# Three interleaved Strassen units in the last two tiles of an attention + SiLU-MLP kernel, with their first copies on VectorE

**Chip, cores, metric.** One core of one Trainium2 (trn2) chip. The metric is the device time of one execution in microseconds; the profiled span is 1.83 us shorter than the time of the same run.

## The reference

Abridged, in the notation of NumPy:

```python
def _attn_ref(q, k, v):                    # B=8, H=8, S=576, D=64, f32
    k_p = k.reshape(B, H, Sp, 8, D).mean(axis=3)        # Sp = 72
    v_p = v.reshape(B, H, Sp, 8, D).mean(axis=3)
    scores = np.matmul(q, k_p.transpose(0, 1, 3, 2)) / np.sqrt(D)
    attn = softmax(scores)                 # (cut)
    return np.matmul(attn, v_p)

def _moe_ref(x, w_in, w_out):              # x: 4608 x 512, w_in: 512 x 2048, w_out: 2048 x 512
    h = x @ w_in
    g = h * (1.0 / (1.0 + np.exp(-h)))
    return g @ w_out
```

## The kernel before

The 4608 tokens are worked off in nine tiles of 512 (t = 0 to 8). Each tile has an *up* phase (x to hidden, 16 groups of 128 hidden features) and a *down* phase (hidden to output). Attention of batch t+1 runs in between the matmuls of tile t; tiles 7 and 8 have none left. In the up phase some groups are *plain* (four matmuls of 512 columns each). Others are done four at a time as a *unit*: one level of Strassen, seven products in place of eight, each of four matmuls of 256 columns. The cost of a unit is its sums: of weights (once, in tile 0), of x (five for each tile), and of products. The products share three banks P, Q, R of PSUM, the memory into which TensorE writes its results. VectorE and ScalarE read them there, so that a product which adds onto a bank has to wait until the bank's last value has been read.

```python
def spread(fillers, n):          # fillers (at, function): run when matmul step `at` has been issued
    todo = sorted(fillers, key=lambda f: f[0])
    for i in range(n):
        yield i
        while todo and todo[0][0] <= i:
            todo.pop(0)[1]()
    for f in todo:
        f[1]()

def stage(y, n):                                     # unit y, Strassen product n
    if n == "2":
        product(y, 2, "P", True)                     # True: the bank is started anew
        nc.scalar.copy(r_sb, ps["P"])                # r, the "first copy"
    elif n == "5":
        product(y, 5, "Q", True)
        tt(out=rr_sb, in0=ps["Q"], in1=r_sb, op=ALU.add)             # rr
    elif n == "1":
        product(y, 1, "R", True)
        tt(out=t_sb, in0=ps["R"], in1=rr_sb, op=ALU.subtract)        # t
    elif n == "4":
        product(y, 4, "P", False)                    # adds onto P: r has to be out
        hidden(y, 1, 0, ps["P"])                     # SiLU on ScalarE
    elif n == "3":
        product(y, 3, "Q", False)                    # adds onto Q: rr has to be done
        hidden(y, 0, 1, ps["Q"])
    elif n == "7":
        product(y, 7, "P", False)                    # adds onto P: SiLU of 4 has to be done
        tt(out=c_sb[0], in0=ps["P"], in1=t_sb, op=ALU.add)           # c0
        hidden(y, 0, 0, c_sb[0])
    elif n == "6":
        product(y, 6, "Q", False)
        tt(out=c_sb[1], in0=ps["Q"], in1=t_sb, op=ALU.add)           # c1
    else:                                            # "s"
        hidden(y, 1, 1, c_sb[1])
```

The order of an up phase in tiles 2 to 8 (G is plain), its x sums and its hidden sums (the sums that the down phase, also Strassen, multiplies):

```python
items = (
    G(12, 13) + [(0, "251")] + G(14) + [(0, "43")] + G(15) + [(0, "76")]
    + [(1, "2")] + [(0, "s")] + [(1, "51")] + G(0) + [(1, "43")] + G(1)
    + [(1, "76")] + G(2) + [(1, "s")] + G(3)
)
for n in U_X:                                        # x sums for products 1, 4, 3, 7, 6
    f_up.append((0, lambda n=n: unit_x_sum(t, n)))
for n in (2, 5):
    f_up.append((36 if t > 1 else 45, lambda n=n: hidden_sum(n, 4, 8)))
f_up.append((56, lambda: hidden_sum(6, 4, 8)))
for n, k0 in ((2, 0), (5, 0), (1, 4), (1, 0)):
    f_up.append((64, lambda n=n, k0=k0: hidden_sum(n, k0, k0 + 4)))
f_down.append((33, lambda: hidden_sum(7, 0, 8)))
f_down.append((71, lambda: hidden_sum(6, 0, 4)))
```

The down phase starts with what needs only the upper half (4 to 8) of the hidden sums:

```python
product(2, KA, KQ)               # KA = 4, KQ = 8
product(5, KA, KQ)
product(2, 0, KA)
nc.scalar.copy(r_sb, ps["P"])
product(5, 0, KA)
tt(out=rr_sb, in0=ps["Q"], in1=r_sb, op=add)
for cc in ((0,), (1,)) if last else ((0, 1),):       # the last tile in two column halves
    product(1, 0, KQ, cc)                            # bank R
    ...                                              # products 4, 3, 7, 6 (cut)
```

The softmax here doesn't subtract the row's maximum and nothing guards it: scores larger than these inputs give would overflow.

Of the kernel before, what the change touches and what calls it, by code (L numbers as in the profile page):

```python
# [27 lines left out]
FP32 = mybir.dt.float32  # L28
FP32R = mybir.dt.float32r
BF16 = mybir.dt.bfloat16  # L30
AX = mybir.AxisListType.X
AF = mybir.ActivationFunctionType
ALU = mybir.AluOpType
# [3 lines left out]
def kernel(  # L37
# [9 lines left out]
    nc = tc.nc  # L47

    B, H, S, D = q.shape
# [11 lines left out]
    KQ, NQ, CQ = KG // 2, NTT // 2, d_model // 2  # L61
# [19 lines left out]
    singles = ctx.enter_context(tc.tile_pool(name="singles", bufs=1))  # L81
# [8 lines left out]
    def ps_tile(shape, dtype, tag, name):  # L90
        return psum.tile(shape, dtype, tag=tag, bufs=banks[tag], name=name)
# [16 lines left out]
    r_sb = singles.tile([128, 2, CQ], FP32, name="r_sb")  # L108
    rr_sb = singles.tile([128, 2, CQ], FP32, name="rr_sb")
    t_sb = singles.tile([128, 2, CQ], FP32, name="t_sb")  # L110
    xT = singles.tile([128, KF, NX], BF16, name="xT")

    w_sum1 = [singles.tile([128, 5, 2, 256], BF16, name=f"w_sum1{n}") for n in range(2)]
    x_sum = singles.tile([128, 5, 2, NQ], BF16, name="x_sum")
    c_sb = [singles.tile([128, 2, NQ], FP32, name=f"c_sb{n}") for n in range(2)]

# [272 lines left out]
    def spread(fillers, n):  # L389
# [7 lines that stand above are left out]



    UNITS = ((4, 6), (8, 10))  # L400
    UW = [
        {
            (i, j): w_in_sb[:, 2 * j : 2 * j + 2, 128 * u : 128 * (u + 2)]
            for i, u in enumerate(us) for j in range(2)
        } for us in UNITS
    ]
# [18 lines left out]
    def unit_x_sum(t, n):  # L425
        a, b = U_X[n]
        nc.vector.tensor_tensor(
            out=x_sum[:, U_XI[n]], in0=x_quarter(t, *a), in1=x_quarter(t, *b),
            op=ALU.subtract if n in (3, 4) else ALU.add,
        )  # L430

    def unit_weights(y, n):
        if n in U_WI:
            return w_sum1[y][:, U_WI[n]]
        return UW[y][0, 0] if n == 3 else UW[y][1, 1]

    def unit_x(t, n):
        if n in U_XI:
            return x_sum[:, U_XI[n]]
        return x_quarter(t, 0, 0) if n == 2 else x_quarter(t, 1, 1)  # L440


    def up(t, fillers, items):
        step = spread(
            fillers,
            sum(
                KF if len(it) == 3 else 2 * len(it[1].strip("s")) for it in items
            ),
        )
        ps = {}  # L450

        def product(y, n, bank, first):
            if first:
                tag = "mm" if bank == "R" else "at"
                ps[bank] = ps_tile([128, 2, NQ], FP32, tag, f"u_ps{bank}")
            w, x = unit_weights(y, n), unit_x(t, n)
            for u in range(2):
                next(step)
                for kk in range(2):
                    nc.tensor.matmul(  # L460
                        ps[bank][:, u, :], lhsT=w[:, kk, 128 * u : 128 * (u + 1)],
                        rhs=x[:, kk, :], start=first and u == 0 and kk == 0,
                        stop=kk == 1, skip_group_check=True,
                    )

        def hidden(y, i, j, src):
            g = UNITS[y][i]
            nc.scalar.activation(  # L468
                h_T[:, g : g + 2, j * NQ : (j + 1) * NQ], src, func=AF.Silu
            )  # L470

        tt = nc.vector.tensor_tensor

        def stage(y, n):
            if n == "2":
                product(y, 2, "P", True)
                nc.scalar.copy(r_sb, ps["P"])
            elif n == "5":
                product(y, 5, "Q", True)
                tt(out=rr_sb, in0=ps["Q"], in1=r_sb, op=ALU.add)  # L480
            elif n == "1":
                product(y, 1, "R", True)
                tt(out=t_sb, in0=ps["R"], in1=rr_sb, op=ALU.subtract)
            elif n == "4":
                product(y, 4, "P", False)
                hidden(y, 1, 0, ps["P"])
            elif n == "3":
                product(y, 3, "Q", False)
                hidden(y, 0, 1, ps["Q"])
            elif n == "7":  # L490
                product(y, 7, "P", False)
                tt(out=c_sb[0], in0=ps["P"], in1=t_sb, op=ALU.add)  # L492
                hidden(y, 0, 0, c_sb[0])
            elif n == "6":
                product(y, 6, "Q", False)
                tt(out=c_sb[1], in0=ps["Q"], in1=t_sb, op=ALU.add)
            else:
                hidden(y, 1, 1, c_sb[1])

        for it in items:  # L500
            if len(it) == 3:
                plain(t, step, *it)
            else:
                for n in it[1]:
                    stage(it[0], n)
        for _ in step:
            pass
# [61 lines left out]
    def quarter(i, j, ks):  # L569
        return h_T[:, j * KQ + ks.start : j * KQ + ks.stop, i * NQ : (i + 1) * NQ]  # L570
# [9 lines left out]
    def hidden_sum(n, k0, k1):  # L580
        a, b, op = H_SUMS[n]
        ks = slice(k0, k1)
        nc.vector.tensor_tensor(  # L583
            out=h_sum[n][:, ks, :], in0=quarter(*a, ks), in1=quarter(*b, ks), op=op
        )
# [166 lines left out]
    def load_half_2(name, half):  # L752
        for i0, i1 in ((0, SA), (SA, SLOTS), (SLOTS, SLOTS + 1)):
            load_slots(nc.gpsimd, 2, name, i0, i1, half)

    visits = [(f, g) for f in range(2) for g in range(2)]
    for t in range(NT):
        a = t + 1
        f_up, f_down = [], []
        if t == 0:  # L760
            GA = 11
            items = [(g, 0, HS) for g in range(GA)]
            items += [(g, HS, NTT - HS) for g in range(GA)]
            items += [(g, 0, NTT) for g in range(GA, KG)]
            f_up += [(1, lambda: denominators(0, 0, 1, on_dve=True))]
            f_up += [(5, lambda: denominators(0, 1, 1, on_dve=True))]
            f_up += [(13, lambda: numerators(0, 0, 1))]
            f_up += [(17, lambda: numerators(0, 1, 1))]
        else:
            G = lambda *gs: [(g, 0, NTT) for g in gs]  # L770
            if t == 1:
                items = (
                    G(12, 13, 14, 15) + [(0, "251")] + G(8) + [(0, "43")] + G(9)
                    + [(0, "76")] + G(10) + [(0, "s")] + G(11, 0, 1, 2, 3)
                )
            else:
                items = (
                    G(12, 13) + [(0, "251")] + G(14) + [(0, "43")] + G(15) + [(0, "76")]
                    + [(1, "2")] + [(0, "s")] + [(1, "51")] + G(0) + [(1, "43")] + G(1)
                    + [(1, "76")] + G(2) + [(1, "s")] + G(3)  # L780
                )
            for n in U_X:
                f_up.append((0, lambda n=n: unit_x_sum(t, n)))
            for n in (2, 5):
                f_up.append((36 if t > 1 else 45, lambda n=n: hidden_sum(n, 4, 8)))
            f_up.append((56, lambda: hidden_sum(6, 4, 8)))
            for n, k0 in ((2, 0), (5, 0), (1, 4), (1, 0)):
                f_up.append((64, lambda n=n, k0=k0: hidden_sum(n, k0, k0 + 4)))
            f_down.append((33, lambda: hidden_sum(7, 0, 8)))
            f_down.append((71, lambda: hidden_sum(6, 0, 4)))  # L790
# [9 lines left out]
        if a < B:  # L800
# [23 lines left out]
            if t == 0:  # L824
                f_down.append((0, lambda: load_half_2("k", 0)))
                f_down.append((0, lambda: load_q(2)))
                f_down.append((0, lambda: load_half_2("k", 1)))
                for half in range(2):
                    f_down.append((31, lambda half=half: load_half_2("v", half)))
                for y in range(2):  # L830
                    for n in U_W:
                        f_down.append((6, lambda y=y, n=n: unit_weight_sum(y, n)))
            elif a + 1 < B:
                for stage in range(2):
                    f_down.append((100, lambda stage=stage: pool_k(a + 1, stage)))
                f_up.append((0, lambda: load_q(a + 1)))
                f_up.append((1, lambda: load_one(a + 1, "k")))
                f_up.append((2, lambda: load_rest(a + 1, "k")))
                f_down.append((11, lambda: load_one(a + 1, "v")))
                f_down.append((12, lambda: load_rest(a + 1, "v")))  # L840
# [51 lines left out]
```

## Time and profile before

| | before |
|---|---|
| time, median (range) | 291.48 us (291.2 to 291.8, 4 runs) |
| span of the profiled run, granted clock | 288.6 us, 0.998 |
| up phase of tiles 7 and 8 | 13.0 us each, TensorE busy 12.9 |
| VectorE busy in it | 9.5 us |
| ScalarE busy in it | 8.8 us |

The lines behind it are in the prediction. In a timeline the first two columns are start and length in us. A row of "x4" is four instructions merged, so its length includes the overlap of matmuls with the next group; the distance from start to start is what a group costs TensorE.

### The profile page before, as it was taken

Reading aid. Unit: us, or ns where it says so; the run is one execution under the profiler, and the core shown is the slowest. Engines: PE = TensorE matmul, PEld = TensorE weight load, DVE = VectorE, ACT = ScalarE, POOL = GpSimd, SP = SyncE. Lnnn points to the kernel's source line nnn. Section 1 sums busy time; section 2 is a strip of 40 time slices with the busy share of each in tenths; the row PEclk is TensorE's granted clock in tenths of the full one; section 3 lists DMA queues with packets and bytes.
Section 4 is the critical chain, followed back from the end, with each engine's and each line's share of the span. In section 5 each row is a group of like instructions: output and inputs, shape, how many; then the busy total and the mean of one; then the engine's idle time right before and its main releaser. Section 6 shows DMA issues by size and latency. Waiting matters only on the chain.

```text
span 288.6 us, 6600 instructions
## 1 busy us (share of the span) xinstructions
PE 281.2 (97%) x2578; PEld 189.9 (66%) x2597; DVE 226.8 (79%) x417; ACT 187.9 (65%) x401; POOL 52.2 (18%) x68
## 2 busy tenths in 40 slices
PE   7989999999999999999999999999999999999995
PEld 2448434465667676657788767676777667786684
DVE  4986844989789796979698879887988876746783
ACT  1768675568656877578767866786679657425700
POOL 8744316501020011101200106203000000000000
PEclk9999999999999999999999999999999999999999
DMA  7999999893758565875995495979830023005004
GB/s 214 276 278 215 232 301 151 221 206 55 145 82 187 127 91 76 133 179 123 137 182 166 61 138 81 164 156 163 149 82 2 2 65 83 1 2 140 6 2 145
DMA packets 35295, 37.67 MB, mean 131 GB/s; under 512 B 9952, under 2 KB 27616, under 8 KB 35264
## 3 DMA queue, kind: packets, MB, share of 16 engines
q0 software_dynamic: 21760, 20.86, 43.3%
q1 hardware_dynamic: 12928, 15.48, 22.0%
q10 hardware_dynamic: 576, 0.92, 0.9%
q8 instruction: 20, 0.33, 0.5%
q14 instruction: 11, 0.09, 0.1%
HBM read 36.70 MB, written 9.44 MB: 160 GB/s over the span
## 4 chain that ended last, share of the span: by engine, by line
PE 91%; DVE 2%; ACT 2%; DMA 2%; issue 1%; DVEq 0%
PE hp_ps L518 24%; PE o_psP L623 15%; PE o_psQ L623 15%; PE u_psQ L460 6%; PE u_psP L460 6%; PE o_psR L623 5%; PE o_ps L550 4%; PE sc_ps L330 4%; PE nu_ps L370 3%; PE den_ps L347 3%; PE u_psR L460 2%; DMA raw<-in_k_dram 2%; PE warm_ps L672 1%; ACT es L338 1%; PE kz_ps L295 1%
## 5 line engine op out<-in xcount | busy, mean ns | idle before, releaser
L518 PE MATMUL hp_ps<-xT,w_in_sb 128*128 128x512 bf16 (+3 forms) x398 | 80.5, 338 | 1.2 <-ACT h_T L524 0.4
L524 ACT ACTIVATE h_T<-hp_ps 128x512 bf16<-128x512 f32 (+2 forms) x95 | 51.4, 545 | 33.1 <-PE hp_ps L518 31.9
L623 PEld LDWEIGHTS <-h_sum 128*128 128x128 bf16 x640 | 60.4, 98 | 15.2 <-issue 6.1
L583 DVE TENSOR_TENSOR h_sum<-h_T 128x1024 bf16<-128x1024 bf16 (+1 forms) x72 | 50.9, 743 | 7.0 <-ACT h_T L524 7.0
L518 PEld LDWEIGHTS <-w_in_sb 128*128 128x128 bf16 x412 | 39.3, 98 | 24.9 <-issue 1.5
L338 ACT ACTIVATE es<-sc_ps 72x288 bf16<-72x288 f32 x128 | 41.4, 402 | 12.6 <-PE sc_ps L330 12.5
L378 DVE TENSOR_TENSOR xT<-nu_ps,rec 128x288 bf16<-128x288 f32 x64 | 25.8, 450 | 13.2 <-PE nu_ps L370 13.0
L460 PEld LDWEIGHTS <-w_sum 128*128 128x128 bf16 x300 | 29.3, 98 | 7.7
L623 PEld LDWEIGHTS <-h_T 128*128 128x128 bf16 x256 | 23.5, 98 | 6.7 <-issue 4.3
L468 ACT ACTIVATE h_T<-c_sb 128x512 bf16<-128x512 f32 x30 | 18.8, 628 | 10.8 <-DVE c_sb L492 10.8
L152 DVE STREAM_TRANSPOSE qT<-q_bf 128x576 bf16<-128x576 bf16 x32 | 22.9, 753 | 0.0
L181 POOL DMA_DIRECT2D raw<-in_k_dram x5 | 7.0, 1405 | 75.1 <-DVE h_sum L583 37.7
L356 ACT ACTIVATE lnd<-den_ps 128x288 f32<-128x288 f32 x30 | 12.3, 411 | 10.8 <-PE nu_ps L370 5.8
L273 DVE TENSOR_TENSOR raw<-raw 128x384 f32<-128x384 f32 (+3 forms) x20 | 12.4, 619 | 8.0 <-DMA raw<-in_v_dram 4.4
L623 PE MATMUL o_psP<-w_out_sb,h_sum 128*128 128x256 bf16 x128 | 17.6, 273 | 0.0
L623 PE MATMUL o_psQ<-w_out_sb,h_sum 128*128 128x256 bf16 x128 | 17.6, 273 | 0.0
L623 PE MATMUL o_psQ<-w_sum,h_T 128*128 128x256 bf16 x128 | 17.5, 274 | 0.0
L623 PE MATMUL o_psP<-w_sum,h_sum 128*128 128x256 bf16 x128 | 17.0, 273 | 0.0
L623 PE MATMUL o_psR<-w_sum,h_sum 128*128 128x256 bf16 x128 | 16.7, 273 | 0.0
L623 PE MATMUL o_psP<-w_sum,h_T 128*128 128x256 bf16 x128 | 16.7, 273 | 0.0
L530 POOL DMA_DIRECT2D out_dram<-o_sb x1 | 0.6, 628 | 82.3 <-issue 82.3
L623 PE MATMUL o_psQ<-w_sum,h_sum 128*128 128x256 bf16 x128 | 15.4, 273 | 0.0
(77 smaller groups left out, 426.8 us busy)
## 6 DMA issues: line engine op xcount, KB each, us to landing
out_dram<-o_sb SPq DMA_DIRECT2D x128, 64.0 KB, 2.5
q_bf<-in_q_dram POOLq DMA_DIRECT2D x6, 576.0 KB, 11.4
raw<-in_k_dram SPq DMA_DIRECT2D x6, 512.0 KB, 5.5
raw<-in_k_dram POOLq DMA_DIRECT2D x5, 576.0 KB, 8.8
raw<-in_v_dram POOLq DMA_DIRECT2D x5, 576.0 KB, 8.7
raw<-in_v_dram SPq DMA_DIRECT2D x5, 512.0 KB, 6.4
w_in_sb<-in_moe_w_in_dram POOLq DMA_DIRECT2D x8, 256.0 KB, 8.7
w_out_sb<-in_moe_w_out_dram POOLq DMA_DIRECT2D x4, 512.0 KB, 13.5
```

The source lines that it names most:

```text
L152: nc.vector.transpose(out=st["qT"][:, a, f * QF : (f + 1) * QF].rearrange("r i c p -> r (i c p)"), in_=st["q_bf"][:, a, f * n : (f + 1) * n],)
L273: nc.vector.tensor_add(out=raw[..., :w], in0=raw[..., :w], in1=raw[..., w : 2 * w])
L330: nc.tensor.matmul(sc[s], lhsT=kz[b % 2][rows, g, c, :], rhs=st["qT"][rows, g, f * QF : (f + 1) * QF, c, :], start=(c == 0), stop=(c == 1),)
L338: nc.scalar.activation(es[:, s, :], sc[s], func=AF.Exp, scale=score_scale)
L356: nc.scalar.activation(lnd, den_ps[:, :HS], func=AF.Ln)
L378: nc.vector.tensor_mul(out=xT[:, 2 * g + c, cols], in0=nu[c][:, :HS], in1=rec)
L460: nc.tensor.matmul(ps[bank][:, u, :], lhsT=w[:, kk, 128 * u : 128 * (u + 1)], rhs=x[:, kk, :], start=first and u == 0 and kk == 0, stop=kk ...
L468: nc.scalar.activation(h_T[:, g : g + 2, j * NQ : (j + 1) * NQ], src, func=AF.Silu)
L518: nc.tensor.matmul(hp_ps[:, r0:r1], lhsT=w_in_sb[:, kk, g * 128 : (g + 1) * 128], rhs=xT[:, kk, x0 : x0 + r1 - r0], start=(kk == 0), stop= ...
L524: nc.scalar.activation(h_T[:, g, n0 : n0 + n], hp_ps[:, :n], func=AF.Silu)
L583: nc.vector.tensor_tensor(out=h_sum[n][:, ks, :], in0=quarter(*a, ks), in1=quarter(*b, ks), op=op)
L623: nc.tensor.matmul(ps[b][:, c, :], lhsT=left(n, kt, c), rhs=W_OUT[n][:, kt, :], start=b not in begun, stop=kt == k1 - 1, skip_group_check= ...
```

## The change

The intent: a third unit takes four more plain groups of tiles 7 and 8, where no attention competes, and saves another eighth of their matmul work. The three units are interleaved so that one's reads of PSUM lie beside another's matmuls, the four groups left fill gaps, and the first copies go to VectorE.

```diff
-    w_sum1 = [... for n in range(2)]
+    w_sum1 = [... for n in range(3)]
-    UNITS = ((4, 6), (8, 10))
+    UNITS = ((4, 6), (8, 10), (12, 14))
     (ps[bank] becomes ps[y, bank] throughout: cut)
-                nc.scalar.copy(r_sb, ps["P"])
+                copy = nc.scalar.copy if t < B - 1 else nc.vector.tensor_copy
+                copy(r_sb, ps[y, "P"])
+            if t >= B - 1:
+                items = (
+                    G(0) + [(0, "251"), (0, "43"), (2, "25"), (0, "76"), (2, "1")]
+                    + [(0, "s"), (2, "43"), (1, "25")] + G(1) + [(2, "76"), (1, "1")]
+                    + [(2, "s"), (1, "43")] + G(2) + [(1, "7")] + G(3) + [(1, "6s")]
+                )
-                f_up.append((36 if t > 1 else 45, lambda n=n: hidden_sum(n, 4, 8)))
+                f_up.append((45 if t == 1 or t >= B - 1 else 36, lambda n=n: hidden_sum(n, 4, 8)))
-                for y in range(2):                   # weight sums, in tile 0
+                for y in range(3):
```

More of the change, by code (lines that the diff above doesn't have):

```diff
@@ L111 @@
     xT = singles.tile([128, KF, NX], BF16, name="xT")
-    w_sum1 = [singles.tile([128, 5, 2, 256], BF16, name=f"w_sum1{n}") for n in range(2)]
+    w_sum1 = [singles.tile([128, 5, 2, 256], BF16, name=f"w_sum1{n}") for n in range(3)]
     x_sum = singles.tile([128, 5, 2, NQ], BF16, name="x_sum")
@@ L454, in product @@
                 tag = "mm" if bank == "R" else "at"
-                ps[bank] = ps_tile([128, 2, NQ], FP32, tag, f"u_ps{bank}")
+                ps[y, bank] = ps_tile([128, 2, NQ], FP32, tag, f"u_ps{bank}")
             w, x = unit_weights(y, n), unit_x(t, n)
@@ L460, in product @@
                     nc.tensor.matmul(
-                        ps[bank][:, u, :], lhsT=w[:, kk, 128 * u : 128 * (u + 1)],
+                        ps[y, bank][:, u, :], lhsT=w[:, kk, 128 * u : 128 * (u + 1)],
                         rhs=x[:, kk, :], start=first and u == 0 and kk == 0,
@@ L476, in stage @@
                 product(y, 2, "P", True)
-                nc.scalar.copy(r_sb, ps["P"])
+                copy = nc.scalar.copy if t < B - 1 else nc.vector.tensor_copy
+                copy(r_sb, ps[y, "P"])
             elif n == "5":
                 product(y, 5, "Q", True)
-                tt(out=rr_sb, in0=ps["Q"], in1=r_sb, op=ALU.add)
+                tt(out=rr_sb, in0=ps[y, "Q"], in1=r_sb, op=ALU.add)
             elif n == "1":
                 product(y, 1, "R", True)
-                tt(out=t_sb, in0=ps["R"], in1=rr_sb, op=ALU.subtract)
+                tt(out=t_sb, in0=ps[y, "R"], in1=rr_sb, op=ALU.subtract)
             elif n == "4":
                 product(y, 4, "P", False)
-                hidden(y, 1, 0, ps["P"])
+                hidden(y, 1, 0, ps[y, "P"])
             elif n == "3":
                 product(y, 3, "Q", False)
-                hidden(y, 0, 1, ps["Q"])
+                hidden(y, 0, 1, ps[y, "Q"])
             elif n == "7":
                 product(y, 7, "P", False)
-                tt(out=c_sb[0], in0=ps["P"], in1=t_sb, op=ALU.add)
+                tt(out=c_sb[0], in0=ps[y, "P"], in1=t_sb, op=ALU.add)
                 hidden(y, 0, 0, c_sb[0])
@@ L495, in stage @@
                 product(y, 6, "Q", False)
-                tt(out=c_sb[1], in0=ps["Q"], in1=t_sb, op=ALU.add)
+                tt(out=c_sb[1], in0=ps[y, "Q"], in1=t_sb, op=ALU.add)
             else:
```

## The prediction

> **What bounds the kernel now.** I read the page's busy line first, then the chain that ended last, then the matmul and VectorE timelines of tile 8's up phase (x to hidden), then the busy time by stretch. The busy line and the chain:
>
> ```profile
> PE 281.2 (97%) x2578; PEld 189.9 (66%) x2597; DVE 226.8 (79%) x417; ACT 187.9 (65%) x401; POOL 52.2 (18%) x68
> ...
> PE 91%; DVE 2%; ACT 2%; DMA 2%; issue 1%; DVEq 0%
> ```
>
> TensorE is busy 97% of the span and 91% of the chain, so any gap that opens in it is paid in full, and work taken from it is gained. The stretches of tile 7 up, tile 8 up, and the first 3.6 us of tile 8's down phase (us from the start; then length, and busy time of PE, weight load, DVE, ACT, POOL):
>
> ```profile
> 234.40:247.40 13.00, 12.89 (x88) 8.61 (x89) 9.49 (x17) 8.79 (x17) 0.00 (x0) 1.00 0.34 82
> 259.70:272.70 13.00, 12.90 (x88) 8.61 (x88) 9.50 (x17) 8.81 (x17) 0.00 (x0) 1.00 0.34 81
> 272.70:276.30 3.60, 3.60 (x34) 3.01 (x33) 2.50 (x5) 1.56 (x3) 0.00 (x0) 1.00 0.00 0
> ```
>
> Tiles 7 and 8 have no attention work beside their up phase. PE never stops there (12.9 of 13.0), VectorE has 3.5 us free, ScalarE 4.2 us. TensorE's pace, from the starts in its timeline (start, length, both us):
>
> ```profile
> 261.43 0.60 PE L460 MATMUL u_psP<-xT,w_sum 128*128 128x256 bf16 x4
> 261.87 0.60 PE L460 MATMUL u_psQ<-xT,w_sum 128*128 128x256 bf16 x4
> 262.31 0.60 PE L460 MATMUL u_psR<-x_sum,w_sum 128*128 128x256 bf16 x4
> 262.74 1.03 PE L518 MATMUL hp_ps<-xT,w_in_sb 128*128 128x512 bf16 x4
> 263.61 0.60 PE L460 MATMUL u_psP<-x_sum,w_in_sb 128*128 128x256 bf16 x4
> ```
>
> A Strassen product (four matmuls of 256 columns) advances PE by 0.437 us (261.43, 261.87, 262.31, 262.74), a plain group (four of 512) by 0.867 (262.74 to 263.61). The 0.60 and 1.03 overlap the next group. The VectorE timeline of the same stretch:
>
> ```profile
> 259.91 0.69 DVE L658 TENSOR_TENSOR o_sb<-o_psQ,t_sb 128x512 f32<-128x512 f32 x1 [1.00 <-PE o_psQ L623]
> 260.52 1.76 DVE L427 TENSOR_TENSOR x_sum<-xT 128x512 bf16<-128x512 bf16 x5
> 262.74 0.69 DVE L480 TENSOR_TENSOR rr_sb<-u_psQ,r_sb 128x512 f32<-128x512 f32 x1 [0.47 <-ACT r_sb L477]
> 263.54 0.69 DVE L483 TENSOR_TENSOR t_sb<-u_psR,rr_sb 128x512 f32<-128x512 f32 x1
> 266.04 0.69 DVE L492 TENSOR_TENSOR c_sb<-u_psP,t_sb 128x512 f32<-128x512 f32 x1 [1.81 <-PE u_psP L460]
> 266.64 0.68 DVE L496 TENSOR_TENSOR c_sb<-u_psQ,t_sb 128x512 f32<-128x512 f32 x1
> ```
>
> Four constants come out of it. Five x sums hold VectorE until 262.2 (pitch (1.76-0.42)/4 = 0.335). An op on 128x512 f32 lasts 0.69 us. Its successor starts 0.61 later if it does not read its result (266.04 to 266.64) and 0.80 later if it does (262.74 to 263.54, t_sb reads rr_sb). An add of a fresh PSUM bank starts 0.70 after the first matmul of its product (265.34 in the PE timeline to 266.04).
>
> **What the Trainium skill says.** "TensorE: Matmul & The Clock Gate", section "Wait — 56ns, not 53.3ns?": a warm matmul costs N/2.4 GHz + about 2.5 ns, so 109 and 216 ns for 256 and 512 columns; the trace agrees (0.437/4 = 109, 0.867/4 = 217). "VectorE: DVE Perf Modes", section "The TRN2 errata": fp32 tensor_tensor is (N+151)/0.96, 691 ns for 512; the trace has 692. Its section "The DRAIN you can't avoid" says that a same-engine read-after-write needs a semaphore; the trace agrees, the dependent add carries a semaphore event and comes 0.19 us later than an independent one. "PSUM — Partial Sum Buffer", "PSUM bank collisions raise a hardware error": a bank has to be guarded by semaphores between engines. So product 4, which accumulates on bank P, has to wait for the copy out of P; no run shows a collision here.
>
> **The change part by part.**
>
> *TensorE work.* 8 plain groups and 14 products, 8x0.867 + 14x0.437 = 13.05 us, become 4 and 21, 3.47 + 9.18 = 12.65. Gain 0.41 per tile, 0.82 in all, if nothing waits.
>
> *Weight sums of the third unit.* Five bf16 ops in tile 0's down phase, 5x0.335 = 1.7 us of VectorE. They come after the ten present ones (32.14 to 35.54), where VectorE then waits 4.19 us for a v load. Cost 0.
>
> *VectorE work.* Per tile one more set of four adds and three copies: 7x0.61 = 4.3 us, plus dependence gaps, on the present 9.5 in a phase of 12.65 us. It becomes full. ScalarE loses two copies, and trades four plain SiLUs for four of the unit's, so it stays near 9.
>
> *The head of the phase.* Now three plain groups (12, 13, 14) give VectorE 2.6 us around the first unit; the change leaves one group ahead and none between the first unit's products. Let 0 be the first matmul of tile 8's up phase (259.70). VectorE is in program order and the x sums are issued after the first matmul, so ahead of the copy. The copy of P starts at 2.50 (0.81 + 5x0.335; P itself is ready at 0.87+0.70 = 1.57) and ends at 3.19; rr runs 3.30-3.99, t 4.10-4.79. PE, with products 2, 5, 1 done at 2.18, waits for the copy with product 4 (3.24 rather than 2.18) and for rr with product 3 (4.04). It is done with product 3 at 4.47 rather than 3.05: **a gap of 1.42 us**.
>
> *The middle.* From 4.47 PE runs u2's 2, 5; u0's 7, 6; u2's 1, 4, 3; u1's 2, 5; G1; u2's 7, 6; u1's 1, 4, 3; G2, and reaches 12.33. VectorE meanwhile: r2 5.17, rr2 5.97, c0 6.58, c1 7.19, t2 7.80, r1 8.41, rr1 9.21, c0 9.98, c1 10.59, t1 11.20. Product 3 of u2 wants rr2 (done 6.66) at 7.10; u1's product 5 wants the fifth "at" bank's successor, u0's P, read by 7.27, at 7.97. No stall, by 0.4 us at the least. At u1's 7 there is one of about 0.15: ScalarE does u2's last SiLU (11.30) before that of u1's 4, which ends at 12.43, so 7 starts at 12.48, G3 at 12.92, 6 at 13.79; the phase ends at 14.22. Against 13.02 now: **+1.20**.
>
> *The tail.* Now the phase ends with two plain groups, and the last unit's outputs are long ready. After the change product 6 of u1 is last: its c1 could start at 14.49, but the hidden sum of 6 is issued before it and starts at 14.23 (c0 of u1 at 13.62 + 0.61), so c1 runs 14.86-15.54, SiLU 15.57-16.20, then four hidden sums in 2.50 us (the trace's figure), 16.23-18.73. The down phase has 1.74 us of work that needs none of them, then waits from 15.96 to 16.96 for the first; the third product kind (R) starts at 18.78, when the fourth sum is done. Now it starts at 276.25, which is 16.55 on this clock. **+2.23 per tile in all**: 1.42 + 0.15 of waits, less 0.41 of work gives 1.16 (1.20 with rounding and the wait latencies), and 1.03 in the tail.
>
> Tile 7 has the same timeline 25.3 us earlier (first matmul 234.41), so the sum is 2 x 2.23 = +4.5 us on the path: 291.53 + 4.5 = 296.0.
>
> **The rivals.** (1) *As intended*: waits fit in the slack and the time falls by 0.82 to 290.7. For it speaks that PE is the bound and VectorE had 3.5 us free; against it that this freedom lies later than 0 to 2.5, where the x sums are. (2) *Only the tail counts*: if the copy somehow ran before the x sums (or did not hold PE), rr would end by 4.0 at latest anyway; best case copy 1.57, no head gap beyond product 3's, giving about +0.4 to +1 per tile, 292.5 to 293.5. The program order speaks against it. (3) *VectorE throughput bound throughout*: if every handover cost 0.1 more than I took, about 19 VectorE ops in a row would add 1 to 2 us per tile beyond mine, 298 to 299. The table's slack of 0.4 us in the middle speaks against the full amount. (4) *Clock or start-up effects*: granted clock is 0.998, a gap of 1.4 us is not long; nothing.
>
> **Range and chances.** The two gaps follow from program order and durations that hardly vary, so I trust sign more than size: the tail could be 0.4 smaller if the hidden sum of 6 slips into an earlier hole, the middle 0.3 larger. I take 295.8 us, range 293.8 to 297.2. Two per cent slower is 297.4, which takes +5.8: chance 0.08. Two per cent faster is 285.7, which not even the ideal saving reaches: 0.01. Within 2%: 0.91.
>
> **What would show it.** In the profile after: in tiles 7 and 8 product 4 of the first unit starts about 3.2 us after the phase's first matmul and product 3 about 4.0, both released by VectorE; the first copy starts right after the x sums; VectorE has little idle time until 11.9; at the start of the down phase PE's weight load waits about 1 us for a hidden sum; R starts about 18.8 us after the phase's first matmul; tile 0 is unchanged. I am wrong if the first copy runs before or among the x sums, if PE's head gap is under 1 us, or if the change to R's start is not near 2.2 us in each tile.

## The result, and the profile after

| | before | after |
|---|---|---|
| time, median | 291.48 us | 295.44 us (294.72 to 295.83, 4 runs) |
| ratio, 95% interval | | 1.0133 (1.011 to 1.0155) |
| up phase, tile 8 | 13.0 us | 14.18 us |
| down phase of tile 8, start to the first matmul on R | 3.52 us | 4.21 us |
| first x sum of tile 7 to that of tile 8 | 25.30 us | 27.12 us |
| first x sum of tile 8 to the last group of matmuls | 23.75 us | 25.58 us |

A ratio is the mean time of one kernel's fast runs over that of the other's fast runs of the same rounds, so it is not quite the ratio of the medians.

The last two rows are *tile lengths*, read off the timelines as differences of start times (tile 7 before: 260.52 - 235.22). They are worth more here than the total, since they exclude the start of the kernel, which varies: in the profile of after, tile 7 begins 1.76 us later than before, 1.0 of that in the first 8 us, where the 19 warm-up matmuls took 7.13 us rather than 5.67. That stretch is not touched by the change. The other 0.75 appears between the first x sums of tiles 3 and 7, whose code is the same: counted from the first matmul of the scores, the x sums of tile 3 begin at 109.15 before and 109.13 after, those of tile 7 at 226.80 and 227.55. The two tile lengths together went up by 1.82 + 1.83 = 3.65 us, which accounts for most of the 3.96 us between the medians; the other 0.3 is within the scatter of runs.

The busy line and the chain of the page after:

```profile
PE 285.1 (97%) x2621; PEld 192.5 (65%) x2621; DVE 237.8 (81%) x436; ACT 186.0 (63%) x397; POOL 52.2 (18%) x68
...
PE 21%; DVE 5%; ACT 1%; issue 0%; DVEq 0%
```

These two lines mislead. TensorE is at 97% as before, since a busy share is taken over the whole span, and the chain's shares add up to only 27%: it breaks off, so it is no proof here. The stretches show it (both up phases; length, then busy time of PE, weight load, VectorE, ScalarE, GpSimd):

```profile
236.17:250.34 14.17, 13.09 (x102) 9.74 (x100) 13.01 (x23) 7.58 (x14) 0.00 (x0) 1.00 0.32 75
263.29:277.47 14.18, 13.10 (x103) 9.76 (x101) 13.02 (x23) 7.58 (x14) 0.00 (x0) 1.00 0.31 75
```

VectorE went from 9.5 of 13.0 us to 13.0 of 14.2. It is now the full engine, and TensorE has over a microsecond idle. What TensorE waits for, over the whole run (total us, times, longest):

```profile
PE u_psP L460 <- DVE r_sb L478: 1.8, 2, 0.9
...
PE o_psP L624 <- DVE h_sum L584: 1.0, 2, 0.5
...
PE u_psQ L460 <- DVE rr_sb L481: 0.4, 2, 0.2
```

Each occurs twice, once in tile 7 and once in tile 8, and none of the three occurs before. TensorE's timeline in tile 8 (first matmul 263.29):

```profile
265.03 0.60 PE L460 MATMUL u_psR<-x_sum,w_sum 128*128 128x256 bf16 x4
266.52 0.60 PE L460 MATMUL u_psP<-x_sum,w_in_sb 128*128 128x256 bf16 x4 [0.89 <-DVE r_sb L478]
267.31 0.60 PE L460 MATMUL u_psQ<-x_sum,w_in_sb 128*128 128x256 bf16 x4 [0.20 <-DVE rr_sb L481]
...
274.72 1.03 PE L519 MATMUL hp_ps<-xT,w_in_sb 128*128 128x512 bf16 x4
275.73 0.60 PE L460 MATMUL u_psP<-x_sum,w_sum 128*128 128x256 bf16 x4
...
278.34 1.04 PE L624 MATMUL o_psQ<-w_out_sb,h_sum 128*128 128x256 bf16 x8
279.87 1.05 PE L624 MATMUL o_psP<-w_out_sb,h_sum 128*128 128x256 bf16 x8 [0.50 <-DVE h_sum L584]
...
281.68 1.05 PE L624 MATMUL o_psR<-w_sum,h_sum 128*128 128x256 bf16 x8
```

The same first matmul on R in the profile of before, where the down phase starts at 272.73 (after: 277.47):

```profile
276.25 1.05 PE L623 MATMUL o_psR<-w_sum,h_sum 128*128 128x256 bf16 x8
```

Read it by pace: a product costs 0.437 us, so product 4 of the first unit (266.52) should have come at 265.47: 1.05 lost. Product 3 (267.31) lost another 0.35. The last unit's product 7 (275.73, due 275.59) lost 0.14. In the down phase product 2's lower half (279.87, due 279.21 at 0.872 per eight matmuls) lost 0.66. The bracket shows less than the pace, since the end of a matmul lies after the start of the next. And VectorE's queue in the same stretch:

```profile
264.10 1.76 DVE L427 TENSOR_TENSOR x_sum<-xT 128x512 bf16<-128x512 bf16 x5
265.78 0.69 DVE L478 COPY r_sb<-u_psP 128x512 f32<-128x512 f32 x1
266.57 0.69 DVE L481 TENSOR_TENSOR rr_sb<-u_psQ,r_sb 128x512 f32<-128x512 f32 x1
267.36 0.69 DVE L484 TENSOR_TENSOR t_sb<-u_psR,rr_sb 128x512 f32<-128x512 f32 x1
268.38 0.69 DVE L478 COPY r_sb<-u_psP 128x512 f32<-128x512 f32 x1 [0.33 <-PE u_psP L460]
269.18 0.69 DVE L481 TENSOR_TENSOR rr_sb<-u_psQ,r_sb 128x512 f32<-128x512 f32 x1
269.79 0.68 DVE L493 TENSOR_TENSOR c_sb<-u_psP,t_sb 128x512 f32<-128x512 f32 x1
270.38 0.68 DVE L497 TENSOR_TENSOR c_sb<-u_psQ,t_sb 128x512 f32<-128x512 f32 x1
271.17 0.69 DVE L484 TENSOR_TENSOR t_sb<-u_psR,rr_sb 128x512 f32<-128x512 f32 x1
...
276.45 0.68 DVE L493 TENSOR_TENSOR c_sb<-u_psP,t_sb 128x512 f32<-128x512 f32 x1
277.05 0.68 DVE L584 TENSOR_TENSOR h_sum<-h_T 128x1024 bf16<-128x1024 bf16 x1
277.74 0.69 DVE L497 TENSOR_TENSOR c_sb<-u_psQ,t_sb 128x512 f32<-128x512 f32 x1
279.12 2.50 DVE L584 TENSOR_TENSOR h_sum<-h_T 128x1024 bf16<-128x1024 bf16 x4 [0.70 <-ACT h_T L468]
```

From the first x sum (264.10) to the end of the last c1 (278.43) the view marks one hole, of 0.33 us. The first copy stands right behind the five x sums, as predicted.

### The profile page after: what moved, and what is told of

Its sections match the earlier page's. It is cut to its first block, busy times and chain, and to the rows that moved or that the text cites. A ratio compares the mean times of both kernels' runs of the same rounds, so it can differ in the third digit from the quotient of the medians.

```text
span 294.0 us, 6694 instructions
## 1 busy us (share of the span) xinstructions
PE 285.1 (97%) x2621; PEld 192.5 (65%) x2621; DVE 237.8 (81%) x436; ACT 186.0 (63%) x397; POOL 52.2 (18%) x68
## 5 line engine op out<-in xcount | busy, mean ns | idle before, releaser
L519 PE MATMUL hp_ps<-xT,w_in_sb 128*128 128x512 bf16 (+3 forms) x380 | 75.0, 337 | 0.4 <-ACT h_T L525 0.4
L525 ACT ACTIVATE h_T<-hp_ps 128x512 bf16<-128x512 f32 (+2 forms) x87 | 46.5, 540 | 29.8 <-PE hp_ps L519 24.2
L519 PEld LDWEIGHTS <-w_in_sb 128*128 128x128 bf16 x380 | 36.2, 98 | 22.0 <-issue 1.5
L460 PEld LDWEIGHTS <-w_sum 128*128 128x128 bf16 x340 | 33.2, 98 | 8.9 <-issue 0.5
L468 ACT ACTIVATE h_T<-c_sb 128x512 bf16<-128x512 f32 x34 | 21.2, 629 | 15.5 <-DVE c_sb L493 15.1
L460 PEld LDWEIGHTS <-w_in_sb 128*128 128x128 bf16 x136 | 13.2, 97 | 7.8 <-issue 4.5
```

The source lines that it names most:

```text
L460: nc.tensor.matmul(ps[y, bank][:, u, :], lhsT=w[:, kk, 128 * u : 128 * (u + 1)], rhs=x[:, kk, :], start=first and u == 0 and kk == 0, stop ...
L468: nc.scalar.activation(h_T[:, g : g + 2, j * NQ : (j + 1) * NQ], src, func=AF.Silu)
L519: nc.tensor.matmul(hp_ps[:, r0:r1], lhsT=w_in_sb[:, kk, g * 128 : (g + 1) * 128], rhs=xT[:, kk, x0 : x0 + r1 - r0], start=(kk == 0), stop= ...
L525: nc.scalar.activation(h_T[:, g, n0 : n0 + n], hp_ps[:, :n], func=AF.Silu)
```

## The experiments

Two readings of this profile are possible. **A**: the waits are local, each costs its own length, and one gets it back by putting TensorE work in front of it. **B**: VectorE's chain, from the x sums to the last c1, has become the pace of the phase, and TensorE's gaps are only where that shows. Every run below was correct against the reference. Tile lengths are from each run's own profile:

| run | ratio to before (95%) | tile 7 | tile 8 |
|---|---|---|---|
| before | 1 | 25.30 | 23.75 |
| after | 1.0133 (1.011 to 1.0155) | 27.12 | 25.58 |
| e4_sums_only | 1.0007 (0.9964 to 1.005) | - | - |
| e5_copies_only | 0.9966 (0.9933 to 0.9999) | 25.30 | 23.79 |
| e1_act_copies | 1.0088 (1.0044 to 1.0132) | 26.77 | 25.23 |
| e3_two_head | 1.0103 (1.0057 to 1.0148) | 27.04 | 25.50 |
| e2_late_x | 1.0073 (1.0042 to 1.0104) | 26.49 | 24.93 |
| e6_tail | 1.0097 (1.006 to 1.0135) | 26.51 | 25.29 |
| e7_all | 0.9967 (0.9943 to 0.9991) | 24.85 | 23.58 |
| e10_dup_after | 1.0163 (1.0129 to 1.0196) | 27.78 | 26.22 |
| e11_dup_e8 | 1.0008 (0.9975 to 1.0042) | 24.84 | 24.05 |
| e8_all_down | 0.9975 (0.9952 to 0.9998) | 24.85 | 24.04 |
| e9_all_dve_copies (= e8) | 1.0009 (0.9974 to 1.0044) | 24.85 | 24.04 |
| e12_split | 0.9996 (0.9963 to 1.0028) | 25.58 | 23.17 |

A warning on the second column: e8 and e9 are the same kernel byte for byte (see below), and their ratios differ by 0.34%. Each run has one profile, so a tile length is a single reading; the two of e8 and e9 agree to 0.01 us. Verdicts under half a per cent therefore rest on the tile lengths.

### The parts of the change alone

**e4_sums_only**, on the kernel before: only the third unit's weight sums.

```diff
-    w_sum1 = [... range(2)]          ->  range(3)
-    UNITS = ((4, 6), (8, 10))        ->  ((4, 6), (8, 10), (12, 14))
-                for y in range(2):   ->  range(3)
```

> The kernel before with only the third unit's weight sums added (five more VectorE ops in tile 0, their results unused). Both theories: ratio to before 1.000 +- 0.002; the five ops run in the hole ahead of the v load (VectorE's wait for it falls from about 4.2 to 2.4 us) and the first up phase of tile 1 starts no later. If the early part of the kernel carries some of the loss, the ratio is 1.001 to 1.003.

Ratio 1.0007: no cost seen, though the interval is wide. Its profiled execution was an outlier (987.54 us, TensorE busy 970 us at a granted clock of 1.0; I can't explain it) and shows nothing on the hole. The profile of after does: its weight sums are 15 in 5.08 us rather than 10 in 3.40, and VectorE's wait for the v load after them fell from 4.19 to 2.43 us. The traces of the other runs settle it: in five of the eleven that carry these sums (e2, e3, e7, e8, e12) tile 7's first x sum comes 226.78 to 226.84 us after the first matmul of the scores, against 226.80 before.

**e5_copies_only**, on the kernel before: only the copies of tiles 7 and 8 on VectorE.

```diff
-                nc.scalar.copy(r_sb, ps["P"])
+                copy = nc.scalar.copy if t < B - 1 else nc.vector.tensor_copy
+                copy(r_sb, ps["P"])
```

> The kernel before with only the two first copies of tiles 7 and 8 moved from ScalarE to VectorE. With two plain groups ahead of the first unit and one between its products the copy (2.50 to 3.19 us after the phase's first matmul) and rr (3.30 to 3.99) are done before products 4 (3.91) and 3 (4.34). Theory of order (what counts is what stands between a product and its read): ratio 1.000, no TensorE wait. Rival, the copies on VectorE are themselves the cost: +0.6 us or more for each tile, ratio 1.004.

Tile lengths 25.30 and 23.79 against 25.30 and 23.75: nothing in tile 7, 0.04 us in tile 8. The engine of the copy costs nothing where two plain groups lie ahead of it and one behind.

**e1_act_copies**, on the changed kernel: the copies back on ScalarE.

```diff
-                copy = nc.scalar.copy if t < B - 1 else nc.vector.tensor_copy
-                copy(r_sb, ps[y, "P"])
+                nc.scalar.copy(r_sb, ps[y, "P"])
```

> The changed kernel with the first copies of tiles 7 and 8 back on ScalarE; three interleaved units as changed. Theory of order: the copy starts 1.57 after the first matmul, product 4 at 2.2, but rr still waits behind the x sums until 2.50, so product 3 starts at 3.24 rather than 4.02; the gap moves partly to the last unit's product 7 (about 0.7 us, its bank read by ScalarE behind a SiLU that waits for VectorE) and the tail stays. Gain against the changed kernel only about 0.3 us per tile: 294.9, ratio to before 1.011. Rival, VectorE's amount of work paces the phase: taking three copies (3 x 0.6 to 0.8 us) off it gains about 2 us per tile, 291.5, ratio 1.000.

0.35 us gained in each tile, of 1.82 lost: the small figure was right and the rival (2 us) wrong. So the placing of the copies is a minor part of the loss. TensorE's waits in tiles 7 and 8 of this run:

```profile
PE u_psQ L460 <- DVE rr_sb L480: 0.9, 2, 0.4
PE u_psP L460 <- ACT h_T L468: 0.9, 2, 0.4
```

The wait for the copy is gone. In its place rr, still behind the x sums, holds product 3, and a SiLU holds the last unit's product 7: in ScalarE's queue the SiLU of product 4 (274.26) comes behind two (from 273.12) that waited for VectorE. The amount of VectorE work alone is therefore not the whole cause either: with three ops of 23 fewer, the handovers between the engines take over (VectorE waits 1.00 and 1.35 us for the copies of the second and the last unit).

### What paces the phase

**e3_two_head**, on the changed kernel: a second plain group at the head, taken from the middle.

```diff
-                    G(0) + [(0, "251"), ...
-                    + [(0, "s"), (2, "43"), (1, "25")] + G(1) + [(2, "76"), (1, "1")]
+                    G(0, 1) + [(0, "251"), ...
+                    + [(0, "s"), (2, "43"), (1, "25"), (2, "76"), (1, "1")]
```

> The changed kernel with group 1 moved from the middle to the head (two plain groups before the first unit). Theory A, the head gap by itself costs its length: the gap before product 4 falls from 1.06 to 0.2 us, and the time by 0.87 us per tile, 293.7, ratio to before 1.008. Theory B, VectorE's chain from the x sums to the last c1 sets the phase, and TensorE's gaps are only where it shows: the head gap falls to 0.2 and a gap of about 0.9 to 1.0 us opens later (before a product 7), R starts 18.4 us after the phase's first matmul as before, time unchanged, 295.4, ratio 1.013.

The tiles are 0.08 us shorter, not 0.87. TensorE in tile 8 of this run:

```profile
264.09 0.60 PE L460 MATMUL u_psR<-x_sum,w_sum 128*128 128x256 bf16 x4
264.71 0.60 PE L460 MATMUL u_psP<-x_sum,w_in_sb 128*128 128x256 bf16 x4
...
269.43 0.60 PE L460 MATMUL u_psQ<-xT,w_sum 128*128 128x256 bf16 x4
270.46 0.60 PE L460 MATMUL u_psP<-x_sum,w_sum 128*128 128x256 bf16 x4 [0.43 <-ACT h_T L468]
```

The gap ahead of product 4 shrank from 1.05 to 0.18 us, and one of 0.59 opened ahead of the second unit's product 7, which now has no plain group in front. Theory B: filling the largest visible gap gained next to nothing. The chain itself says the same. From tile 8's first x sum to the start of its last c1 it takes 13.64 us in the changed kernel and 13.55 here; in e10 below it takes 14.27, in e2 12.99, in e1 13.28, and the tile's length follows it within 0.02 us.

**e10_dup_after**, on the changed kernel: one VectorE op of the chain doubled in each of the two tiles.

```diff
                 tt(out=t_sb, in0=ps[y, "R"], in1=rr_sb, op=ALU.subtract)
+                if y == 2:
+                    tt(out=t_sb, in0=ps[y, "R"], in1=rr_sb, op=ALU.subtract)
```

> The changed kernel with one VectorE op doubled: t of the second unit in each of tiles 7 and 8 is computed twice (same operands, same result; 0.61 us of pitch, nothing else changed). Theory B, VectorE's own chain paces the phase: every op added to it lengthens the phase by its pitch, R starts 19.0 us after the first matmul rather than 18.4, +1.2 us in all, 296.6, ratio to before 1.0175. Rival, TensorE's waits at the head and the tail are local and there are 0.4 us of slack in the middle, as the prediction's middle part had it: +0.2 us per tile at most, ratio 1.0145 or less.

Tiles 0.66 and 0.64 us longer: the added op is paid in full. TensorE pays at a place far from the op, ahead of the last unit's product 7, which waits for a SiLU:

```profile
PE u_psP L460 <- ACT h_T L468: 1.3, 2, 0.6
```

The run that separates the two theories is e3. The price here agrees with B, but it can also be had from the prediction's own timeline: that has little slack after this op and a wait of 0.15 before the same product 7, so the "+0.2 us at most" of the expectation did not follow from it.

**e11_dup_e8**: the same doubled op in the repaired kernel e8 (below).

> The same doubled op in the repaired kernel (run e8_all_down), where by the worked-out timeline VectorE is ahead of TensorE. Theory B holds only where VectorE is the pace: here nothing is lost, no TensorE wait appears, and the first x sums of tiles 7 and 8 are 24.85 us apart as in e7_all; ratio to before 0.996. Rival, any VectorE work costs its time once three units run: +0.6 us per tile, ratio 1.000.

24.84 and 24.05 against 24.85 and 24.04 of e8: it costs nothing there. (The expected ratio of 0.996 was missed, at 1.0008. That is within the scatter: e9, at 1.0009, is the kernel that gave 0.9975 as e8.) A VectorE op has no price of its own; it has one where VectorE is the pace.

### Shortening the chain without taking work away

**e2_late_x**, on the changed kernel: the last three x sums issued later.

```diff
+            x_at = (0, 0, 7, 7, 9) if t >= B - 1 else (0, 0, 0, 0, 0)
-            for n in U_X:
-                f_up.append((0, lambda n=n: unit_x_sum(t, n)))
+            for at, n in zip(x_at, U_X):
+                f_up.append((at, lambda n=n: unit_x_sum(t, n)))
```

> The changed kernel with the x sums for products 3, 7 and 6 issued later (after steps 7, 7 and 9 of the phase rather than step 0), so that the first copy stands behind two x sums and not five. No work is taken from VectorE. Theory of order: the copy starts at 1.57 us, product 4 at 2.3, product 3 at 3.25 us after the phase's first matmul, and the phase is 0.6 to 0.76 us shorter per tile: about 294.0, ratio to before 1.009. Rival, the amount of VectorE work: time unchanged, ratio 1.013.

0.63 and 0.65 us gained per tile, the VectorE ops being the same. This is the largest single step of order: the first copy no longer stands behind the sums that nobody needs yet, and the sums fall into two holes of the chain, the 0.19 us by which t waits for its rr and the 0.4 us by which the second unit's copy came late because TensorE was late (0.33 in the bracket above). It is not the best placing. A new wait opened, on a sum now issued too late: product 4 starts at 263.65 and product 3 1.13 us after it.

```profile
264.78 0.60 PE L460 MATMUL u_psQ<-x_sum,w_in_sb 128*128 128x256 bf16 x4 [0.53 <-DVE x_sum L427]
```

**e6_tail**, on the changed kernel: more work in the down phase that does not need the last unit.

```diff
+            late = t >= B - 1
-            f_up.append((56, lambda: hidden_sum(6, 4, 8)))
+            (f_down if late else f_up).append((34 if late else 56, lambda: hidden_sum(6, 4, 8)))
             for n, k0 in ((2, 0), (5, 0), (1, 4), (1, 0)):
-                f_up.append((64, lambda n=n, k0=k0: hidden_sum(n, k0, k0 + 4)))
+                at = 45 if late and k0 else 64
+                f_up.append((at, lambda n=n, k0=k0: hidden_sum(n, k0, k0 + 4)))
         product(5, KA, KQ)
+        if t >= B - 1:
+            product(1, KA, KQ)
         product(2, 0, KA)
-            product(1, 0, KQ, cc)
+            product(1, 0, KA if t >= B - 1 else KQ, cc)
```

> The changed kernel with the down phase of tiles 7 and 8 given work that needs no output of the last unit: hidden sum 1 (upper half) issued early, product 1's upper half put between product 5's upper half and product 2's lower half, hidden sum 6 (upper half) moved into the down phase. The up phase is untouched. If the tail wait is a cost of its own: the 0.50 us wait before product 2's lower half and the later start of R go, product 4 of the down phase starts about 0.5 us earlier per tile (19.6 rather than 20.1 us after the phase's first matmul); 294.4, ratio to before 1.010. If it only takes up slack that VectorE makes elsewhere: unchanged, 1.013.

0.61 us gained in tile 7 and 0.29 in tile 8. The tail is a cost of its own: the chain of the up phase is as long as in the changed kernel (13.63 us against 13.64). In tile 8 a part came back as a new wait; there the columns are split, so product 3 comes eight steps sooner:

```profile
PE o_psQ L624 <- DVE rr_sb L641: 0.3, 1, 0.3
```

### A version that keeps the saving

**e7_all**, on the changed kernel: copies on ScalarE, late x sums, the tail of e6, and another order.

```diff
+                    [(0, "25")] + G(0) + [(0, "143"), (2, "25"), (0, "76"), (2, "143"), (1, "25")]
+                    + [(0, "s")] + G(1) + [(2, "76"), (1, "1"), (2, "s"), (1, "43")]
+                    + G(2, 3) + [(1, "76s")]
+            x_at = (0, 0, 7, 11, 12) if t >= B - 1 else (0, 0, 0, 0, 0)
     (upper halves of hidden sums 2, 5 and 1 at step 41; the rest as in e1, e2 and e6)
```

> Three units with all three repairs: copies on ScalarE, late x sums, the units interleaved so that each read of a bank has at least one product in between, and the tail of the run e6_tail. By the timeline worked out from the measured durations TensorE never waits in the up phase (12.63 us) nor at the start of the down phase; product 4 of the down phase starts 17.9 us after the phase's first matmul against 18.3 before. If the matmul saving of 0.41 us per tile is real, 290.7, ratio to before 0.997. If VectorE or ScalarE cannot carry three units at all, R or product 4 comes later than 18.3 and the ratio is above 1.000.

Tile 7 is 24.85 us, 0.45 under before, and tile 8 is 23.58, 0.17 under. The stretches of the two up phases in this run:

```profile
234.99:247.61 12.62, 12.52 (x100) 9.78 (x100) 10.74 (x20) 9.12 (x17) 0.00 (x0) 1.00 0.35 84
259.84:272.46 12.62, 12.52 (x100) 9.79 (x100) 10.74 (x20) 9.12 (x17) 0.00 (x0) 1.00 0.35 83
```

12.62 us is the bare matmul work (12.65 from the pace in the prediction), with VectorE at 10.7. So three units fit, and the 0.41 us that the change set out to save are real. The run makes four edits at once, and which of them are needed is not shown, except that e12 (below) puts copies on VectorE back into tile 7 and loses 0.73 us. What remains in tile 8 is a wait of 0.3 us for rr in the down phase, as in e6. By time the run beats both kernels: 290.47 us median, ratio 0.9967 with an interval below 1; given the scatter above, the gain of 0.6 us in the tile lengths is the firmer figure.

**e8_all_down**: e7 with hidden sums 6 and 7 of the down phase moved.

```diff
-            (f_down if late else f_up).append((34 if late else 56, lambda: hidden_sum(6, 4, 8)))
+            (f_down if late else f_up).append((3 if late else 56, lambda: hidden_sum(6, 4, 8)))
-            f_down.append((33, lambda: hidden_sum(7, 0, 8)))
-            f_down.append((71, lambda: hidden_sum(6, 0, 4)))
+            (tiles 7 and 8: (2, 7 upper half), (41, 7 lower half), (50, 6 lower half))
```

> The run e7_all with the hidden sums of 6 and 7 in the down phase of tiles 7 and 8 split and moved into VectorE's gaps, so that the last tile's product 3 no longer waits for rr (0.26 us in e7_all), and with hidden sum 6 of the last tile issued before its first use. Expected: no TensorE wait from the first matmul of tile 7 to the end but for what the split columns cost; the last tile 0.3 us shorter; 290.2, ratio to before 0.9955. If the last tile is bound by something else, as e7_all: 0.9967.

A miss: tile 8 became 0.46 us longer than in e7. The wait for rr went, and product 7 now waited for the copy of P, 0.7 us by the waits view, since a moved sum (278.40) stood ahead of that copy (279.00). One thing in passing: the lower half of hidden sum 6 is issued at step 71, but the last tile, split by columns, multiplies its first columns with it from step 64 on. By program order the kernels before and after, and every run but e8, e9, e11 and e12, use there the sum of the tile before (in the profile of before the sum starts at 281.32 and that product at 279.90). The results pass the comparison all the same, so passing does not show that the order is right.

**e9_all_dve_copies** was to be e8 with the copies on VectorE. My edit did not take, and what ran was e8 once more.

> The repaired kernel (run e8_all_down) with the first copies left on VectorE as in the change. Theory: copy, rr and the third x sum now stand in one queue in the head, so product 3 of the first unit waits about 0.7 us for its x sum and the tiles are 0.7 us longer each: x sums 25.6 us apart, ratio to before 1.001. Rival, once the order is repaired it does not matter which engine copies: 24.85, ratio 0.996.

It says nothing on the copies. As a repeat it shows the scatter: identical tile lengths, 0.34% apart in ratio.

**e12_split**: the order of e7, copies on VectorE in tile 7 and on ScalarE in tile 8, and a third placing of the down phase's sums.

```diff
+                copy = nc.scalar.copy if t != B - 1 else nc.vector.tensor_copy
+            f_up.append((60 if late else 56, lambda: hidden_sum(6, 4, 8)))
+            (tiles 7 and 8: (2, 7 upper half), (3, 7 lower half), (53, in tile 7 50, 6 lower half))
```

> Two questions in one kernel, read by tile. e9_all_dve_copies turned out to be e8_all_down byte for byte (the edit did not take), so the copies are tried here, in tile 7 alone: the order of e7_all, tile 7's first copies on VectorE, tile 8's on ScalarE. Theory: in tile 7 product 3 of the first unit waits about 0.7 us, and the first x sums of tiles 7 and 8 are about 25.6 us apart rather than 24.85 (before: 25.30); rival, the engine of the copies does not matter: 24.85. Second, the down phase has hidden sum 6 (upper half) issued after the last c1, where VectorE waits 0.7 us for a SiLU anyway, both halves of hidden sum 7 ahead of rr, and hidden sum 6 (lower half) of the last tile after the copy of P. Theory: no TensorE wait is left in tile 8, and from its first x sum to its last group of matmuls it takes 23.2 us (before 23.75, e7_all 23.58, e8_all_down 24.04); rival, the split columns of the last tile leave VectorE too little time whatever the order: 23.6 or more. In all about 0.3 us under before: ratio 0.999.

Both came out: 25.58 and 23.17 us. With the copies on VectorE tile 7 loses 0.73 us even in the repaired order:

```profile
236.94 0.60 PE L460 MATMUL u_psP<-x_sum,w_in_sb 128*128 128x256 bf16 x4
238.07 0.60 PE L460 MATMUL u_psQ<-x_sum,w_in_sb 128*128 128x256 bf16 x4 [0.53 <-DVE x_sum L427]
```

Product 3 comes 1.13 us after product 4 rather than 0.44. Tile 8 is 0.58 us shorter than before with no TensorE wait left. Copies on ScalarE in both tiles would make 24.85 + 23.17, an estimate of 1.03 us under before; it was not run.

## Why the prediction was right

The forecast was 295.8 us and the measurement 295.44, inside the range. By its steps:

- *TensorE work, gain 0.41 per tile*: right. In e7, which has no TensorE wait in its up phases, they take 12.62 us against 13.02.
- *Weight sums, cost 0*: right. The hole that was to take them shrank by 1.76 us, and tile 3 begins no later (109.13 against 109.15).
- *Head of the phase*: product 4 at 3.24 and product 3 at 4.04 were forecast; 3.23 and 4.02 measured. The gap is 1.40, forecast 1.42.
- *Middle*: one stall of 0.15 before the last unit's product 7; measured 0.14.
- *Tail, +1.03*: mis-sized, 0.69 measured (4.21 - 3.52, nearly all of it the 0.66 before product 2's lower half). The slip is one term: the last unit's c0 was put at 13.62, counted from the start of the group G3 after product 7 and not of product 7 itself. From product 7 (12.48 forecast) it is 13.18; measured 13.16. So the hidden sum of 6 and the last c1 came 0.4 us earlier (c1 at 14.45, not 14.86), and R at 18.39, not 18.78. The prediction had allowed for a tail 0.4 smaller, but for another reason, an earlier hole into which this sum might slip.
- *Sum*: +2.23 per tile forecast, 1.83 measured. By the start of R it is 1.85 (18.39 against 16.54 before), where the prediction had said that it would be wrong if this were not near 2.2. Twice the difference is 0.8 us, of which the forecast total had already rounded off 0.2; the remaining 0.3 us between the tile lengths and the medians helped it by luck.
- *ScalarE*: "stays near 9" was wrong, 7.58 us in the up phase; two copies of 0.58 less are 7.6. Nothing hung on it.
- *Rivals*: the saving as intended (290.7) was refuted. "Only the tail counts" was refuted too: the first copy came behind the x sums, and with the copies on ScalarE (e1) the tiles still lose 1.47 us and not 0.4 to 1. The granted clock was 1.00 in both stretches. "VectorE throughput bound throughout" was set aside as a further loss from longer handovers. The handovers were not longer; but in its plain sense, VectorE's chain as the pace, that rival was the truth, and the prediction listed the same loss as TensorE waits without saying so. Its sums come out the same, its advice would not: from "a gap of 1.42 us" at the head one would have put a plain group there, and e3 shows that this gains 0.08. What shortens the phase is a shorter chain (e2), not a filled gap.

What stays open: the 0.3 us outside tiles 7 and 8, which the scatter of runs does not resolve, and the outlier of e4.

## What to carry to other kernels

A change that trades matmuls for sums has to be priced on the engine that does the sums, in the stretch concerned: write that engine's queue out in program order with its start-to-start distances, and look at what the first op that TensorE needs stands behind. A visible TensorE gap is worth its length only if filling it does not leave the other engine's chain as long as before; a run that fills the gap tells the two apart (e3), and doubling one op of the chain shows whether its ops are paid for (0.66 us in e10, nothing in e11). Hold independent ops (x sums here) back into the holes of a dependent chain rather than issuing them all ahead of it.

## What the Trainium skill lacked or had wrong

- "VectorE: DVE Perf Modes", section "The DRAIN you can't avoid", says of eight copies in a row that "the semaphore costs nothing extra here". Here an independent op of 128x512 f32 follows after 0.60 us (269.79 to 270.38), within the 0.68 of the one before, and one that waits for its predecessor's result after 0.79 (265.78 to 266.57). The same 0.79 is paid where t overwrites what c1 has just read (270.38 to 271.17). No page gives this price of a dependence, 0.19 us; the second and the last unit pay it twice each, 0.4 us, and the first unit twice (r to rr, rr to t).
- "TensorE: Matmul & The Clock Gate", section "Back-to-back issue gap", gives about 131 ns per matmul of 512 columns as the sustained rate with weight loads in between. This case's streams run at 217 ns (0.867 us for four), which is the page's formula for the isolated gap.
- No page gives the time from the first matmul of a group of four (256 columns) to the first op of another engine that reads its bank: 0.70 us here (265.34 to 266.04 in the profile before).
